# First head pair: two more blocks from unstacked parts, rotation of the rest on GpSimd, and the first weight conversion spread over later steps

## The chip, the cores and the metric

The kernel runs on one core of a Trainium2 chip. The metric is the time of one execution on the device, in microseconds (us), as the median of several runs. The core has five engines that work side by side: TensorE (PE, matrix products and transposes), VectorE (DVE), ScalarE (ACT), GpSimd (POOL) and SyncE (SP, which here only issues transfers). Each runs its own instructions in order and waits on semaphores for the others.

## The reference

Attention over 4 batches of 8 heads, 576 positions of 64 values, with rotated Q and K, and then a gated feed-forward layer over the 2304 rows of 512 values that attention gives. All of it is float32.

```python
q_rot, k_rot = (rotate(q), rotate(k))
scores = scale * np.matmul(q_rot, k_rot.transpose(0, 1, 3, 2))
scores = scores - np.max(scores, axis=-1, keepdims=True)
attn = np.exp(scores)
attn = attn / (np.sum(attn, axis=-1, keepdims=True) + 1e-09)
x = np.matmul(attn, v)            # then heads side by side: (2304, 512)
g = x @ w_gate
out = (g * (1.0 / (1.0 + np.exp(-g))) * (x @ w_val)) @ w_out
```

## The kernel before

**Tiling.** The 32 heads are taken as 16 pairs. A pair has nine blocks of scores: blocks 0 to 7 are four groups of 128 queries for either head in turn, block 8 holds the last 64 queries (the tails) of both heads. Blocks are numbered through, n = 9p + b, so block 9 is the first of pair 1. TensorE works on a fast float32 form, so each operand is split into a high and a low part, and a product of two operands is three products: high by high, low by high, high by low.

**A pair's way.** `load_qk` (L180) brings Q, K and the tails into a tile X, `load_v` (L195) brings V into VR. The rotation (`rope`, L198, its inner `part`, L206) is done in three groups: 0 is Q, 1 is K, 2 the tails. A group is four elementwise operations: two with the sines (L224, half the width each), one with the cosines (L227) and one addition (L228). `qk_T` (L291) transposes a group on TensorE, ScalarE writes the high part (`qk_hi`, L317), VectorE subtracts for the low part (`qk_lo`, L320), both into the tile N. `qk_stack` (L324) then copies parts of N by eight transfers into the stacked tiles QK, QZ and BD, in which high and low parts stand above one another, so that one product over 128 rows does the work of two over 64. `vsplit` (L284) makes the high and the low part of V on GpSimd.

**A block's way.** `scores` (L339) makes the products of a block: in the first pair the blocks below `ndir` straight from N, three terms of 64 rows (six instructions); the others from the stack (four instructions; block 8 six). `peak` (L367, the reduction at L375) takes the negated row maxima on VectorE, `exp` (L377, L393) the exponentials with their sums on ScalarE, `trans` (L416) transposes them on TensorE, ScalarE and VectorE again write high and low parts (L437, L438). `tails` (L440) does so for the last columns and queues the products with V, which `pv_some` (L503) hands out, so many a step, as `PLAN["pv"]` says; `pv_evac` copies a finished sum out. Two score buffers, three transpose buffers and one for the products with V exist.

**The start.** `start` (L238) does the first two blocks by hand, in an order that is kept on all engines: VectorE rotates K and then the first quarter of Q, GpSimd the tails; TensorE transposes them, with warm-up products between; then VectorE rotates the other three quarters of Q, blocks 0 and 1 are scored, the rest of Q is transposed, and the stack is copied, three of its six large copies from ScalarE's queue and the rest from SP's.

**The steps.** Then follows one step per block number n (the loop behind L1080). In a step the functions named in `PLAN["order"]` are called: `qk` transposes the next pair's groups at the blocks in `qk0`/`qk`, `scores` and `exp` belong to block n + 1, `trans` to block n - 1, `rope` rotates the pair after the next at block 1, `vsplit` stands at block 8. GpSimd keeps the written order throughout. On TensorE, ScalarE, VectorE and SP a planner puts the instructions in order by its own estimate of times, with the written order as the priority; only instructions wrapped in `keep_in_program_order` are pinned. One group of pair 1's rotation (K) is given to VectorE (`rv=[[1, 1]]`) and called at step 2.

**Weights and inputs of the second part.** `wfirst` (L748) loads one of the first two weight tiles (gate, value) and gives nine conversion steps each (`bits9`, L717): six on VectorE, one on ScalarE, two on GpSimd. `cl` says at which block numbers the loads are made, `cvs` at which of them the eighteen steps are called. The loads go to the single buffer R of `r_p`. In the later pairs the same buffer takes the reciprocal sums (`rload`, L619), four chunks at once, by which `xprep` (L641) on GpSimd multiplies the attention results that come back from memory.

Behind the attention part, up to the end, TensorE does the feed-forward products, with a hand-kept order on all engines.

## Time and profile before

| what | value |
|---|---|
| median of 3 runs | 727.87 us (725.9 to 728.76) |
| the profiled execution | 726.62 us, its span 724.8 us |
| TensorE busy in the span | 699.9 us (97%) |
| VectorE busy | 550.2 us (76%) |
| GpSimd busy | 465.8 us (64%) |
| ScalarE busy | 405.6 us (56%) |
| mean granted clock of TensorE | 0.989 of full speed |

The span runs from the first to the last instruction; what lies around it makes up the rest of the execution's time. A share of busy time is a mean over stages with different limits, so the start of the kernel is read by itself: by stretches of the span, by the chain of waits that ends there, and by the instructions in order of time. The maxima of the blocks (L375) serve as landmarks, since every block has one.

### The profile page before, as it was taken

Reading aid. Unit: us, or ns where it says so; the run is one execution under the profiler, and the core shown is the slowest. Engines: PE = TensorE matmul, PEld = TensorE weight load, DVE = VectorE, ACT = ScalarE, POOL = GpSimd, SP = SyncE. Lnnn points to the kernel's source line nnn. Section 1 sums busy time; section 2 is a strip of 40 time slices with the busy share of each in tenths; the row PEclk is TensorE's granted clock in tenths of the full one; section 3 lists DMA queues with packets and bytes.
Section 4 is the critical chain, followed back from the end, with each engine's and each line's share of the span. In section 5 each row is a group of like instructions: output and inputs, shape, how many; then the busy total and the mean of one; then the engine's idle time right before and its main releaser. Section 6 shows DMA issues by size and latency. Waiting matters only on the chain.

```text
span 724.8 us, 12728 instructions
## 1 busy us (share of the span) xinstructions
PE 699.9 (97%) x4356; PEld 658.8 (91%) x4356; DVE 550.2 (76%) x898; ACT 405.6 (56%) x884; POOL 465.8 (64%) x462
## 2 busy tenths in 40 slices
PE   7699999999999999998989999999999999999997
PEld 6589999999999999997989999999999877888887
DVE  5899888888888889657988868777766894365451
ACT  2688888888888888447543443414334342432331
POOL 5696989999899957576976766556764757200000
PEclk9899999999999999999999999999999999999999
DMA  5887778789887886793347564745547974786671
GB/s 172 223 198 222 200 195 240 199 205 251 217 205 207 229 203 202 201 262 124 118 143 199 162 191 134 202 147 175 161 145 229 305 263 158 291 290 234 203 218 30
DMA packets 111585, 144.12 MB, mean 199 GB/s; under 512 B 17808, under 2 KB 86432, under 8 KB 111520
## 3 DMA queue, kind: packets, MB, share of 16 engines
q1 hardware_dynamic: 106816, 137.51, 66.1%
q10 hardware_dynamic: 4704, 5.79, 2.4%
q8 instruction: 35, 0.57, 0.3%
q14 instruction: 30, 0.25, 0.1%
HBM read 76.61 MB, written 42.54 MB: 164 GB/s over the span
## 4 chain that ended last, share of the span: by engine, by line
PE 69%; DVE 13%; DMA 8%; ACT 6%; issue 1%; POOL 1%; SPq 1%; ACTq 0%; DVEq 0%
PE ch L822 28%; PE ch L939 13%; PE pv L476 10%; PE sc L360 9%; PE tr L436 7%; DMA HF<-hf 2%; DVE nmt L375 2%; PE tr L299 2%; ACT E L393 1%; DMA ht<-sv 1%; DVE HF L880 1%; ACT N L318 1%; POOL fl L695 1%; DMA QZ<-N 1%; DMA hg<-ht 1%
## 5 line engine op out<-in xcount | busy, mean ns | idle before, releaser
L375 DVE TENSOR_REDUCE nmt<-sc 128x1 f32<-128x576 f32 x144 | 107.9, 751 | 19.7 <-PE sc L360 18.4
L393 ACT ACTIVATE E<-sc,nmt 128x576 f32<-128x576 f32 x128 | 97.4, 761 | 9.7 <-DVE nmt L375 8.3
L436 PE MATMUL tr<-ident,E 128*128 128x128 f32 x512 | 77.2, 274 | 0.6 <-DVE N L322 0.6
L806 POOL TENSOR_TENSOR u<-u,z 128x384 f32<-128x384 f32 x30 | 30.5, 1016 | 73.2 <-DVE sg L806 70.8
L360 PE MATMUL sc<-QK 128*128 128x288 f32 x248 | 61.9, 331 | 4.2 <-DMA QK<-N 2.8
L436 PEld LDWEIGHTS tr<-ident,E 128*128 128x128 f32 x512 | 61.7, 141 | 2.6 <-PE tr L299 1.3
L825 ACT COPY c<-ch 128x384 f32<-128x384 f32 x30 | 14.4, 480 | 83.9 <-PE ch L822 49.4
L224 POOL TENSOR_TENSOR t<-X,tabs 128x256 f32<-128x256 f32 (+1 forms) x90 | 52.0, 600 | 14.4 <-DMA X<-in_qk_dram 7.2
L695 DVE TENSOR_TENSOR hl<-hg,hh 128x384 fp32r<-128x384 f32 x44 | 25.8, 587 | 39.2 <-ACT hh L695 39.2
L360 PE MATMUL sc<-N,QZ 128*128 128x288 f32 x248 | 54.0, 300 | 0.7 <-DMA QZ<-N 0.7
L939 PE MATMUL ch<-Oh,hh 128*128 128x512 f32 (+1 forms) x144 | 54.0, 375 | 0.1
L437 ACT CAST ET2h<-tr 128x512 fp32r<-128x512 f32 x80 | 47.1, 589 | 12.4 <-PE tr L436 12.4
L939 PE MATMUL ch<-Oh,hl 128*128 128x512 f32 (+1 forms) x144 | 53.9, 374 | 0.0
L939 PE MATMUL ch<-Ol,hh 128*128 128x512 f32 (+1 forms) x144 | 53.8, 374 | 0.0
L438 DVE TENSOR_TENSOR ET2l<-tr,ET2h 128x512 fp32r<-128x512 f32 x80 | 53.0, 682 | 0.6 <-ACT ET2h L437 0.6
L438 DVE TENSOR_TENSOR ET1l<-tr,ET1h 128x512 fp32r<-128x512 f32 x64 | 42.8, 685 | 7.5 <-ACT ET1h L437 7.4
L228 POOL TENSOR_TENSOR rot<-rot,t 128x512 f32<-128x512 f32 (+1 forms) x45 | 45.8, 1018 | 3.5
L437 ACT CAST ET1h<-tr 128x512 fp32r<-128x512 f32 x64 | 36.4, 598 | 18.2 <-PE tr L436 15.0
L360 PEld LDWEIGHTS sc<-QK 128*128 128x128 f32 x248 | 38.7, 193 | 8.1 <-ACT E L393 4.9
L806 DVE TENSOR_TENSOR sg<-ch,u 128x384 f32<-128x384 f32 x60 | 33.4, 557 | 16.2 <-PE ch L822 13.3
L227 POOL TENSOR_TENSOR rot<-X,tabs 128x512 f32<-128x512 f32 (+1 forms) x45 | 45.5, 1012 | 0.0
L695 ACT CAST hh<-hg 128x384 fp32r<-128x384 f32 x44 | 22.6, 514 | 38.8 <-DVE hg L926 38.8
(411 smaller groups left out, 2420.3 us busy)
## 6 DMA issues: line engine op xcount, KB each, us to landing
QK<-N SPq DMA_DIRECT2D x62, 288.0 KB, 5.0
hg<-ht SPq DMA_DIRECT2D x22, 768.0 KB, 6.1
HF<-hf SPq DMA_DIRECT2D x12, 896.0 KB, 5.1
X<-in_qk_dram SPq DMA_DIRECT2D x15, 576.0 KB, 6.7
yd<-Y SPq DMA_DIRECT2D x31, 256.0 KB, 4.0
ht<-sg SPq DMA_DIRECT2D x20, 384.0 KB, 3.6
hf<-sg SPq DMA_DIRECT2D x20, 384.0 KB, 3.6
ht<-sg SPq DMA_DIRECT2D x20, 320.0 KB, 2.9
```

The lines of the kernel that those rows point to most:

```text
L224: ins = e.tensor_tensor(out=sel(t2, u), in0=sel(x, w), in1=tb(Sn, u), op=ALU.mult)
L360: nc.tensor.matmul(ps[:, g, 0:288], l, rr[:, o + g * 288:o + (g + 1) * 288], start=(x == 0), stop=(x == len(terms) - 1))
L375: nc.vector.tensor_reduce(out=nmcol, in_=ps[:, :, 0:288], axis=AX.XY, op=ALU.max, negate=True)
L393: nc.scalar.activation(out=E.rearrange("p (a b) -> p a b", a=2), in_=ps[:, :, 0:288], func=ACTF.Exp, bias=nmcol, scale=1.0, accum_out=self ...
L436: nc.tensor.transpose(ps[:, c], E[:, o + c * 128:o + (c + 1) * 128], self.ident)
L437: nc.scalar.copy(dst[0], src)
L438: nc.vector.tensor_tensor(out=dst[1], in0=src, in1=r32(dst[0]), op=ALU.subtract)
L476: nc.tensor.matmul(st["ps"][:, 0:w], VS[:, sl, :], t, start=(x == 0), stop=(x == last))
L695: return [lambda: self.nc.scalar.copy(h, f), lambda: le.tensor_tensor(out=l, in0=f, in1=r32(h), op=ALU.subtract)]
L806: add = lambda e, out, in0, in1: e.tensor_tensor(out=out, in0=in0, in1=in1, op=ALU.add)
L822: nc.tensor.matmul(acc, l[:, w, c * 128:(c + 1) * 128], r, start=(n == 0), stop=(n == 5))
L939: self.nc.tensor.matmul(ps, l[:, f], r[:, z], start=(n == 0), stop=(n == 3 * NFF - 1))
```

## The change

- `ndir` goes from 4 to 6: blocks 4 and 5 of pair 0 are also made from the unstacked parts.
- In the start, the other three quarters of Q of pair 0 are rotated by GpSimd, behind the tails. The group of pair 1 that VectorE had goes to GpSimd too; GpSimd takes pair 1's groups in the order Q, tails, K, later pairs' in the order tails, Q, K.
- V is loaded ahead of pair 1's X. Pair 2's X is loaded inside the start, before the stack copies. The stack copies are all issued by SP.
- The high part of V of pair 0 is copied by ScalarE in the start; GpSimd makes the low part only.
- In the start, ScalarE writes the high part of the rest of Q before its first exponential.
- In the first nine steps TensorE too keeps the written order (`ctl1`), and the products with V are handed out by a list of their own (`pv0`): ten at step 6, ten at step 7, two at step 8.
- Pair 1's groups are transposed at blocks 3, 4 and 5 (Q, tails, K) of pair 0, pair 2's at blocks 1, 2 and 3 of pair 1.
- The conversion of the first weight tiles: loads at blocks 9 and 67 and not 0 and 9; the eighteen steps between blocks 12 and 104 and not 2 and 28.
- The reciprocal sums are loaded in halves of two chunks into a buffer of their own (`Rh`); R stays with the weight tiles up to block 104.

```diff
-    ndir=4,
+    ndir=6,
-    rv=[[1, 1]],
-    rl=2,
-    qk0=[2, 4, 4],
-    qk=[0, 0, 1],
-    qkw0=[0, 1, 2],
-    qkw=[2, 0, 1],
+    qk=[[3, 4, 5], [1, 2, 3], [0, 0, 1]],
+    qkw=[[0, 2, 1], [2, 0, 1], [2, 0, 1]],
     pv=[1, 6, 5, 3, 7, 8, 2, 7, 3],
+    pv0=[0, 0, 0, 0, 0, 0, 10, 10, 2],
-    cl=[0, 9],
-    cvs=[2, 2, 3, 3, 4, 4, 5, 6, 8, 12, 14, 16, 18, 20, 22, 24, 26, 28],
+    cl=[9, 67],
+    cvs=[12, 18, 24, 30, 36, 42, 48, 54, 60, 72, 76, 80, 84, 88, 92, 96, 100, 104],
...
+    def rope(self, p, order=(2, 0, 1)):
+        self.rot[p] = self.rot_p.tile([128, NSLOT, D], FP32, name="rot")
+        for g in order:
+            self.turn(self.nc.gpsimd, p, g)
+        del self.X[p]
...
-        for x in STARTS[PLAN["st"]]:
-            part((ve, po)[x[0]], *x[1:])
+        self.turn(ve, 0, 1)
+        self.turn(po, 0, 2)
+        self.turn(ve, 0, 0, 0, 1)
+        self.turn(po, 0, 0, 1, 4)
...
+        nc.scalar.copy(self.VS[0][:, :, 0:64], self.VR)
         warm(PLAN["warm"][1])
-        part(ve, 0, 0, 2, 1, 4, own=False)
...
         warm(PLAN["warm"][3])
+        hi(ps[:, 128:512], 192, 384)
         self.exp(0)
         self.peak(1)
-        hi(ps[:, 128:512], 192, 384)
         lo(ps[:, 128:512], 192, 384)
         self.exp(1)
+        del self.rot[0], self.X[0]
+        self.load_qk(2)
         self.qk_stack(0)
-        del self.rot[0]
...
-        nc.gpsimd.tensor_scalar(out=VS[:, :, 0:64], in0=VR, scalar1=1.0, scalar2=1.0, op0=ALU.mult, op1=ALU.mult)
+        if p:
+            nc.gpsimd.tensor_scalar(out=VS[:, :, 0:64], in0=VR, scalar1=1.0, scalar2=1.0, op0=ALU.mult, op1=ALU.mult)
...
-        e = d if p else self.nc.scalar.dma_start
-        e(out=QK[U, 1], in_=pair(N[V, 0, 0:576], QH + 576))
-        e(out=QK[V, 1], in_=pair(N[V, 1, 0:576], 576))
-        e(out=QZ[V, 1], in_=N[V, 1, 64:576])
+        d(out=QK[U, 1], in_=pair(N[V, 0, 0:576], QH + 576))
+        d(out=QK[V, 1], in_=pair(N[V, 1, 0:576], 576))
+        d(out=QZ[V, 1], in_=N[V, 1, 64:576])
...
         at.load_qk(0)
+        at.load_v(0)
         at.load_qk(1)
-        at.load_v(0)
         at.start()
-        at.load_qk(2)
...
-    at.rope(1)
+    at.rope(1, (0, 2, 1))
...
-        at.pv_some(P["pv"][b])
+        at.pv_some(P["pv" if p else "pv0"][b])
...
-            if c == 0:
-                moe.rload(s, t)
+            if c % 2 == 0:
+                moe.rload(s, t, at.rh_p.tile([128, 2 * BK], FP32, name="Rh"), c, 2)
...
+    ctl1 = tc.manual_schedule(engines={mybir.EngineType.PE})
+    ctl1.__enter__()
     for n in range(NB):
         p, b = divmod(n, 9)
+        if n == 9:
+            ctl1.__exit__(None, None, None)
```

## Rows read from the trace of the kernel before

**Rows 1.** Chain of waits, first 60 us: start us, us, what.

```profile
8.94 0.42 DVE Et L224
9.36 0.60 DVE rot L227
...
11.03 0.53 DVE t L224 x2
...
12.06 0.56 DVE rot L228
...
16.00 6.16 DMA QZ<-N
```

**Rows 2.** Instructions in order of time, first 46 us: start us, us, engine, line.

```profile
6.98 0.78 POOL L228 TENSOR_TENSOR rot<-rot,t 128x128 f32<-128x128 f32 x1
...
12.76 1.41 POOL L224 TENSOR_TENSOR t<-X,tabs 128x256 f32<-128x256 f32 x2 [5.00 <-DVE rot L228]
...
14.12 1.28 POOL L227 TENSOR_TENSOR rot<-X,tabs 128x512 f32<-128x512 f32 x1
...
15.44 1.17 PE L360 MATMUL sc<-N 64*128 64x288 f32 x12
...
16.81 0.66 PE L299 MATMUL tr<-ident,rot 128*128 128x128 f32 x4 [0.20 <-POOL rot L228]
16.83 0.60 POOL L224 TENSOR_TENSOR t<-X,tabs 128x64 f32<-128x64 f32 x2
...
18.35 0.72 POOL L288 TENSOR_SCALAR VS<-VR 128x640 fp32r<-128x640 f32 x1
...
19.69 0.59 ACT L318 CAST N<-tr 128x512 fp32r<-128x512 f32 x1
...
20.31 0.69 DVE L322 TENSOR_TENSOR N<-tr,N 128x512 fp32r<-128x512 f32 x1 [0.52 <-ACT N L318]
...
20.69 0.82 PE L360 MATMUL sc<-QK 128*128 128x288 f32 x2 [2.79 <-DMA QK<-N]
...
26.11 2.00 POOL L224 TENSOR_TENSOR t<-X,tabs 128x256 f32<-128x256 f32 x2 [5.41 <-DMA X<-in_qk_dram]
```

**Rows 3.** VectorE in order of time: maxima of blocks 9, 18, 36, 54.

```profile
36.74 0.74 DVE L375 TENSOR_REDUCE nmt<-sc 128x1 f32<-128x576 f32 x1
...
54.68 0.74 DVE L375 TENSOR_REDUCE nmt<-sc 128x1 f32<-128x576 f32 x1
...
87.52 0.76 DVE L375 TENSOR_REDUCE nmt<-sc 128x1 f32<-128x576 f32 x1 [0.21 <-PE sc L360]
...
120.80 0.76 DVE L375 TENSOR_REDUCE nmt<-sc 128x1 f32<-128x576 f32 x1 [0.21 <-PE sc L360]
```

**Rows 4.** Stretches: length, busy us of each engine, TensorE clock, DMA share, GB/s.

```profile
10.00:40.00 30.00, 22.52 (x155) 19.32 (x154) 24.19 (x39) 15.88 (x39) 20.43 (x24) 0.89 0.66 178
46.00:63.00 17.00, 16.45 (x128) 15.50 (x127) 16.72 (x26) 14.42 (x38) 16.37 (x19) 1.00 0.84 210
63.00:80.00 17.00, 16.86 (x135) 16.39 (x135) 16.25 (x27) 15.46 (x40) 10.69 (x14) 1.00 0.69 180
114.00:131.00 17.00, 16.89 (x135) 16.48 (x134) 14.94 (x24) 15.13 (x40) 15.54 (x19) 1.00 0.83 209
```

**Rows 5.** Stretches, TensorE alone: length, busy us, granted clock, DMA share, GB/s.

```profile
17.00:20.20 3.20, 0.90 (x8) 0.96 1.03 280
20.20:27.00 6.80, 5.53 (x21) 0.52 0.94 263
```

**Rows 6.** Transfer issues, first 50 us: count, KB each, median us to landing.

```profile
QK<-N SPq DMA_DIRECT2D x10, 288.0 KB, 4.3
```

**Rows 7.** SP in order of time, 112 to 114 us.

```profile
112.87 1.49 SPq L334 DMA_DIRECT2D QK<-N  x1
```

**Rows 8.** Groups by line, VectorE, first 46 us: busy us, mean ns.

```profile
L738 DVE SCALAR_TENSOR_TENSOR R<-R 128x512 uint32<-128x512 uint32 x1 | 1.6, 1616 | 0.0
...
L739 DVE TENSOR_SCALAR R<-R 128x512 uint32<-128x512 uint32 x1 | 0.6, 578 | 0.0
```

More of the change, by code (lines that the diff above doesn't have):

```diff
@@ new lines, in turn @@
+    def turn(self, e, p, g, ra=0, rz=4):
+        X, rot = self.X[p], self.rot[p]
+        C, Sn = self.tab[:, 0], self.tab[:, 1]
+        m = rz - ra
+        if e is self.nc.vector:
+            tt = self.et_p.tile([128, 640], FP32, name="Et")[:, 0:512].rearrange("p (s d) -> p s d", d=D)
+        else:
+            tt = self.t_p.tile([128, 8, D], FP32, name="t2")
+        if g < 2:
+            x = X[:, 8 * g:8 * g + 8].rearrange("p (h r) d -> p h r d", r=4)[:, :, ra:rz]
+            o = rot[:, 8 * g:8 * g + 8].rearrange("p (r h) d -> p h r d", h=2)[:, :, ra:rz]
+            tb = lambda t, u: t[:, None, 5 - 5 * g + ra:5 - 5 * g + rz, u].to_broadcast([128, 2, m, u.stop - u.start])
+            t2 = tt[:, 0:m * 2].rearrange("p (h r) d -> p h r d", r=m)
+            sel = lambda t, u: t[:, :, :, u]
+        else:
+            x, o = X[:, 16:18], rot[:, 16:18]
+            tb = lambda t, u: t[:, 4:5, u].to_broadcast([128, 2, u.stop - u.start])
+            t2 = tt[:, 0:2]
+            sel = lambda t, u: t[:, :, u]
+        for u, w in ((slice(0, HALF), slice(HALF, D)), (slice(HALF, D), slice(0, HALF))):
+            e.tensor_tensor(out=sel(t2, u), in0=sel(x, w), in1=tb(Sn, u), op=ALU.mult)
+        e.tensor_tensor(out=o, in0=x, in1=tb(C, slice(0, D)), op=ALU.mult)
+        e.tensor_tensor(out=o, in0=o, in1=t2, op=ALU.add)
@@ L617, in aux, with rload @@
         return self.aux_p.tile([128, 512], FP32, name="aux")
-    def rload(self, s, t, into=None):
-        R = self.r_p.tile([128, NCH * BK], FP32, name="R") if into is None else into
-        R = R.rearrange("p (c n) -> p c n", c=NCH)
+    def rload(self, s, t, R, c0=0, nc=NCH):
+        R = R.rearrange("p (c n) -> p c n", c=nc)
         b0, b1 = 2 * s, 2 * s + 1
```

62 lines of the change are left out of this document (10 added, 52 removed), and 4 rows, old and new, of the table STARTS.

## The prediction

> **What bounds the kernel now.** I read the stretches first, then the chain of waits, then the timeline of the first 46 us. In a stretch from the middle of the attention part TensorE is busy for 16.89 of 17.00 us [rows 4]: from there on nothing but TensorE's own work sets the time, and an edit elsewhere is free as long as it fits beside. The first pair differs. From 10 to 40 us TensorE is busy for 22.52 of 30 us [rows 4], warm-up products included, so 7.48 us are idle. The row maxima show the same: between the first maximum of pair 1 (block 9) and that of pair 2 (block 18) lie 54.68 - 36.74 = 17.94 us, while the two pairs from block 18 to block 36 take 87.52 - 54.68 = 32.84, or 16.42 each [rows 3]. At that pace a block costs 16.42 / 9 = 1.83 us. Pair 1 is thus 1.52 over the pace, and pair 0 ends far over it.
>
> The chain of waits names the causes in pair 0. Up to the first maximum it is VectorE: two operations of pair 1's K rotation have slid in between (8.94 to 9.96), and the rest of pair 0's Q rotation stands ahead of the maximum (11.03 to 12.62) [rows 1]. Then it is the stacked copies: 6.16 us for the QZ copy issued at 16.00, which lands at 22.16 [rows 1], with TensorE idle for 2.79 us before block 4 at 20.69 [rows 2]. The clock falls behind that idleness: granted 0.52 from 20.2 to 27.0, nearly all of it at the lower level of 1.2 GHz, after a stretch in which TensorE had been busy for 0.90 of 3.20 us [rows 5]. After that the conversion of the first weight tiles fills VectorE: 16.72 of 17 us from 46 to 63 [rows 4].
>
> **The change, part by part.** I count back from the landmark of block 9's maximum (36.74) and block 18's (54.68), since behind block 18 TensorE is full and a shift there is carried to the end.
>
> *Start.* Off VectorE go the two slid operations, 0.42 + 0.60 = 1.02, and the rest of Q, from 11.03 to 12.06 + 0.56 = 12.62, 1.59 [rows 1]. The chain could shrink by 2.61, at the least by 1.02. Blocks 2 and 3 start at 15.44 [rows 2]; they now wait for the rest of Q from GpSimd. That price the trace does not show at this size. GpSimd takes 1.41 / 2 = 0.70 for 128x256 and 1.28 for 128x512 [rows 2], so by size two operations of 128x192 cost 0.53 each and two of 128x384 0.96 each: 2.98, behind the tails' turn that ends at 6.98 + 0.78 = 7.76. That gives 10.74; behind it still stand three transposes and the eight warm-up products. I take 1.7 of gain, block 2 at 13.7 (bounds 12.8 and 14.4). The copy of V's high part on ScalarE lies where the chain is VectorE's throughout [rows 1], with ScalarE waiting for the first maximum, and costs nothing; without that cover it costs one operation, about the 0.72 of GpSimd's own copy at 18.35 [rows 2]. Loading V ahead of pair 1's X delays that X, but GpSimd reads it from 10.7 on only.
>
> *Blocks 4 and 5 from parts.* Twelve products of the unstacked form took 1.17 us for two blocks [rows 2], so a block is about 0.6 to 0.7; four products more than from the stack, some 0.3 us in all. In return the wait of 2.79 and the one for QZ go. The stack is first needed at block 6. At the steady pace that is 13.7 + 4 x 1.83 = 21.0. The three copies that leave ScalarE's queue stand behind three others on SP, and behind the load of pair 2's X, which itself waits for GpSimd's 10.74. With 4.3 us from issue to landing as the median [rows 6] and 6.16 as the slow case the copies for block 6 land between 19 and 21.5: at most half a microsecond is lost. What is late next is pair 1.
>
> *Pair 1 from GpSimd.* All three groups are now GpSimd's, in its order: 10.74 + Q group (0.70 + 0.70 + 1.28 + 1.28 = 3.96) + tails (16.83 to 18.35, 1.52) + K group (3.96) = 20.2 [rows 2]; with some lengthening, since the same two operations took 2.00 at 26.11 and 1.41 at 12.76, I take 20.8. Then four transposes (0.66), the high part (0.59), the low part (0.69) [rows 2], on SP one copy ahead of the low part's (about 0.6) and 4.3 from issue to landing [rows 6]: 27.6. With half a microsecond for the queue it is 28.1 for block 9, and its maximum at 28.8. By pace alone block 9 would be reached at 13.7 + 7 x 1.83 = 26.5, so this chain, not TensorE, is what is late. Against 36.74 that gives 8.0 us. Bounds: the pace, 27.2, gives 9.5; GpSimd's 12 us stretched by a fifth (2.4) and 6.16 for the landing (1.9) give 33.1, or 3.6.
>
> *Pair 1 itself* took 17.94 with conversion steps on VectorE; only one step of eighteen is left in it, at block 12. Between 16.42 and 17.94 I take 17.4, another 0.5 (bounds 0 and 1.5). Pair 2's X is issued before the stack and not at 20 us, so GpSimd need not wait for it before 26.11 [rows 2]; its 9.4 us of rotation end near 32, when pair 1 asks for it at its blocks 1 to 3.
>
> *Conversion over pairs 1 to 11.* Eighteen steps, of which twelve are VectorE's, four GpSimd's. They cost nothing as long as VectorE has room: 14.94 of 17 us are used in the middle [rows 4], 2.06 are free, and a pair gets one and a half to two steps. In favour: from 63 to 80 VectorE was busy for 16.25 of 17 us and those pairs kept the pace of 16.42. *The halved loads of the reciprocals* wait for GpSimd's multiplication of the chunk before; behind them on SP stand stores and the next stack. Pair 6's last stack copy is issued at 112.87 [rows 7] and its first maximum comes at 120.80 [rows 3], so SP has some 4 us of room after landing: nothing.
>
> Sum: 8.0 + 0.5 = 8.5 us (bounds 3.6 and 11.0). The profiled execution took 726.62, its span 724.8; the median of the runs, 727.87, is 1.25 above it. 726.62 - 8.5 = 718.1, beside the median 719.4, which I forecast.
>
> **One rule against the change.** GpSimd's operations are stretched at times: the same two took 1.41 at 12.76 and 2.00 at 26.11, 0.59 more [rows 2]. The Trainium skill, page "SBUF — State Buffer", section "SBUF: two separate sides", gives a reason: GpSimd and VectorE share a port pair, which is an exclusive lock for a whole instruction when VectorE reads two operands from SBUF; whoever comes second waits. By that rule GpSimd's turn of the rest of Q, which begins beside VectorE's four operations on Q's first quarter, would wait perhaps twice; at 0.59 each, an estimate, that makes 1.2, and the sum would be 7.3, 720.6 beside the median. VectorE's later work in the first pair reads one operand from PSUM, so the rule asks no more there. I leave the sum as it is.
>
> **Rivals.** (a) The wait moves. TensorE, held in written order, stands before block 9 as it stood before block 4, and the clock falls again. Nearly 7 us at the lower level in a stretch that is otherwise full cost half of it, 3.4 us: 8.5 - 3.4 = 5.1, 722.8. For it: the wait before block 9 in my own count is 1.6 us. Against it: it is shorter than the 2.79, with products on either side.
> (b) The written order eats the gain. Before, the planner could put ready products of P and V into a gap; now nothing may overtake the transposes that wait for GpSimd, and the 7.48 us of idleness stay as they are, only elsewhere. Then only the start's 1.7 to 2.6 are left: 725.3 to 726.2, no change that shows. Against it: GpSimd begins 2.0 us earlier than its first turn of pair 1 at 12.76 and does not stop for X.
> (c) Slower: the conversion lands on TensorE's path. Each of the twelve VectorE steps takes 0.58 to 1.62 [rows 8], 1.1 as the middle, and if each delays a maximum while TensorE has nothing else queued, pairs 1 to 11 lose 12 x 1.1 = 13.2: 727.87 - 8.5 + 13.2 = 732.6. It decides from where a step is longer than what VectorE has free between two maxima, 2.06 / 9 = 0.23 a block if nothing is queued ahead; the two score buffers speak against it, and the pairs from block 18 on, which carried steps at the full pace.
>
> **How the numbers follow.** Forecast 719.4, with 717 to 721.5 for itself: 0.60. (a), or the lower bounds of pair 1's chain (3.6 gives 724.3): 0.20. (b): 0.11. (c): 0.09. A measurement of this kernel tells apart about 0.5%, 3.6 us. The forecast and (a) lie beyond that on the fast side: 0.80; (b) is within: 0.11; (c) slower: 0.09. The range goes from 716.5 (the whole of 11.0 us) to 724.3 and leaves out (b) and (c).
>
> **What would show it.** Right: block 2 near 13.7, no wait on a QK or QZ copy before block 4, block 9's maximum at 28 to 30, block 18's at 45 to 47, later pairs at 16.4 to 16.7, granted clock full after 20 us. Wrong: TensorE waiting long for GpSimd's rotation or a QK copy before block 9 (then (a) or (b)); pairs 2 to 11 over 17 us with VectorE's conversion lines as the releaser (then (c)).

## The result and the profile after

The changed kernel takes 735.9 us (median; 732.2 to 738.0), the kernel before 727.6 beside it: a ratio of 1.011 [1.0065, 1.0156]. It is slower by 8.3 us where I had forecast 8.5 us of gain.

The maxima of the blocks tell where. VectorE in order of time, the kernel after, the maxima of blocks 9, 18, 108, 135 and 143 (the last), beside [rows 3]; then the kernel before, blocks 108, 135 and 143:

```profile
35.68 0.76 DVE L355 TENSOR_REDUCE nmt<-sc 128x1 f32<-128x576 f32 x1 [2.51 <-PE sc L340]
...
56.44 0.76 DVE L355 TENSOR_REDUCE nmt<-sc 128x1 f32<-128x576 f32 x1 [0.49 <-PE sc L340]
...
225.94 0.76 DVE L355 TENSOR_REDUCE nmt<-sc 128x1 f32<-128x576 f32 x1 [0.21 <-PE sc L340]
...
275.55 0.76 DVE L355 TENSOR_REDUCE nmt<-sc 128x1 f32<-128x576 f32 x1 [0.20 <-PE sc L340]
...
295.08 0.74 DVE L355 TENSOR_REDUCE nmt<-sc 128x1 f32<-128x576 f32 x1
```

```profile
219.80 0.76 DVE L375 TENSOR_REDUCE nmt<-sc 128x1 f32<-128x576 f32 x1 [0.21 <-PE sc L360]
...
269.39 0.76 DVE L375 TENSOR_REDUCE nmt<-sc 128x1 f32<-128x576 f32 x1 [0.20 <-PE sc L360]
...
285.69 0.74 DVE L375 TENSOR_REDUCE nmt<-sc 128x1 f32<-128x576 f32 x1
```

Between the two profiled executions (spans 734.1 and 724.8, 9.3 apart) the account is:

| stretch, by maxima | before | after | difference |
|---|---|---|---|
| up to block 9 | 36.74 | 35.68 | -1.06 |
| pair 1 (blocks 9 to 18) | 17.94 | 20.76 | +2.82 |
| pairs 2 to 11 | 165.12 | 169.50 | +4.38 |
| pairs 12 to 14 | 49.59 | 49.61 | +0.02 |
| pair 15, to its block 8 | 16.30 | 19.53 | +3.23 |
| behind the last maximum | 439.11 | 439.02 | -0.09 |

**The start.** Instructions in order of time, after, with what ended the wait ahead of them in brackets:

```profile
7.98 0.76 DVE L207 TENSOR_TENSOR Et<-X,tabs 128x64 f32<-128x64 f32 x2 [0.59 <-DMA tabs<-in_rope_dram]
8.05 1.16 POOL L207 TENSOR_TENSOR t<-X,tabs 128x192 f32<-128x192 f32 x2 [0.34 <-DMA tabs<-in_rope_dram]
8.66 0.69 DVE L208 TENSOR_TENSOR rot<-X,tabs 128x128 f32<-128x128 f32 x1
9.17 1.04 POOL L208 TENSOR_TENSOR rot<-X,tabs 128x384 f32<-128x384 f32 x1
9.39 0.97 DVE L209 TENSOR_TENSOR rot<-rot,Et 128x128 f32<-128x128 f32 x1
...
10.41 0.33 PE L241 MATMUL tr<-ident,rot 128*128 128x128 f32 x1 [1.68 <-DVE rot L209]
...
19.00 1.06 PE L340 MATMUL sc<-N 64*128 64x288 f32 x6
...
19.74 1.27 POOL L209 TENSOR_TENSOR rot<-rot,t 128x512 f32<-128x512 f32 x1
...
26.06 0.60 PE L280 MATMUL tr<-ident,rot 128*128 128x128 f32 x4
...
34.88 0.50 PE L340 MATMUL sc<-QK 128*128 128x288 f32 x2 [1.86 <-DMA QK<-N]
...
37.42 0.82 PE L340 MATMUL sc<-QK 128*128 128x288 f32 x2 [1.03 <-DMA QK<-N]
```

VectorE's four operations on Q's first quarter and GpSimd's on the rest end in turn: GpSimd's first pair ends at 9.21, VectorE's operation from 8.66, whose like took 0.28 before, at 9.35; GpSimd's next ends at 10.21, VectorE's at 10.36. VectorE takes 2.38 us for the four. TensorE waits 1.68 us for it. Block 2, forecast at 13.7, begins at 19.00. Then blocks 2 to 8 run without a wait on a stack copy, as intended, and blocks 9 and 10 each wait for a QK copy (1.86 and 1.03 us). GpSimd ends pair 1's last group, K, at 21.01; the transposes of that group stand at block 5 in TensorE's written order and come only at 26.06, and the QK copies are issued behind them.

Stretches, after (length, busy us of the engines, granted clock, share of the transfer engines, GB/s), in the order PE, PEld, DVE, ACT, POOL:

```profile
11.90:18.80 6.90, 6.90 (x35) 6.12 (x34) 1.98 (x3) 1.94 (x5) 6.59 (x11) 0.52 0.32 101
24.70:34.90 10.20, 8.00 (x63) 7.19 (x61) 7.34 (x13) 7.99 (x21) 9.88 (x12) 1.00 0.95 229
35.80:42.70 6.90, 5.87 (x27) 5.44 (x26) 4.17 (x7) 3.45 (x9) 6.66 (x8) 0.52 0.37 122
```

The clock is at the lower of its two levels, 1.2 GHz, twice: behind the wait for VectorE's quarter and behind the wait before block 9. In the first stretch TensorE is busy throughout, but mostly with products at half speed. Before there was one such stretch [rows 5].

### The profile page after: what moved, and what is told of

Same layout as the page of the kernel before. It is cut to its first block, busy times and chain, and to the rows that moved or that the text cites. A ratio compares the mean times of both kernels' runs of the same rounds, so it can differ in the third digit from the quotient of the medians.

```text
span 734.1 us, 12779 instructions
## 1 busy us (share of the span) xinstructions
PE 704.9 (96%) x4360; PEld 662.7 (90%) x4360; DVE 546.9 (74%) x890; ACT 408.4 (56%) x885; POOL 470.9 (64%) x469
## 3 DMA queue, kind: packets, MB, share of 16 engines
q1 hardware_dynamic: 107344, 138.24, 66.1%
## 4 chain that ended last, share of the span: by engine, by line
PE 75%; DVE 8%; DMA 7%; ACT 4%; SPq 2%; issue 2%; POOL 1%; ACTq 0%; DVEq 0%
PE ch L801 27%; PE ch L918 12%; PE pv L456 10%; PE sc L340 10%; PE tr L416 7%; PE ch L869 3%; DMA HF<-hf 2%; PE ch L753 2%; PE tr L280 2%; DVE nmt L355 1%; DMA ht<-sv 1%; DMA raw<-in_moe_w_gate_dram 1%; ACT E L373 1%; DVE ET2l L418 1%; DVE HF L859 1%
## 5 line engine op out<-in xcount | busy, mean ns | idle before, releaser
L373 ACT ACTIVATE E<-sc,nmt 128x576 f32<-128x576 f32 x128 | 97.1, 759 | 11.1 <-DVE nmt L355 10.2
L804 ACT COPY c<-ch 128x384 f32<-128x384 f32 x30 | 14.4, 480 | 83.9 <-PE ch L801 45.7
L207 POOL TENSOR_TENSOR t<-X,tabs 128x256 f32<-128x256 f32 (+2 forms) x94 | 54.2, 599 | 4.5 <-DMA X<-in_qk_dram 1.7
L417 ACT CAST ET2h<-tr 128x512 fp32r<-128x512 f32 x80 | 47.1, 589 | 16.2 <-PE tr L416 15.7
L209 POOL TENSOR_TENSOR rot<-rot,t 128x512 f32<-128x512 f32 (+2 forms) x47 | 47.7, 1015 | 3.7
L208 POOL TENSOR_TENSOR rot<-X,tabs 128x512 f32<-128x512 f32 (+2 forms) x47 | 47.5, 1010 | 0.0
L785 DVE TENSOR_TENSOR sg<-ch,u 128x384 f32<-128x384 f32 x60 | 33.4, 557 | 16.2 <-PE ch L801 13.0
```

Of the source, the lines that this page charges most:

```text
L207: e.tensor_tensor(out=sel(t2, u), in0=sel(x, w), in1=tb(Sn, u), op=ALU.mult)
L373: nc.scalar.activation(out=E.rearrange("p (a b) -> p a b", a=2), in_=ps[:, :, 0:288], func=ACTF.Exp, bias=nmcol, scale=1.0, accum_out=self ...
L417: nc.scalar.copy(dst[0], src)
L785: add = lambda e, out, in0, in1: e.tensor_tensor(out=out, in0=in0, in1=in1, op=ALU.add)
```

## The experiments

All medians stand beside the kernel before on the same chip (726.7 to 727.9). Landmarks are of the profiled execution: first maximum, those of blocks 9 and 18, and the time of pairs 2 to 11 and of pair 15.

| run | median us | ratio to before | first | block 9 | block 18 | pairs 2-11 | pair 15 |
|---|---|---|---|---|---|---|---|
| before | 727.6 | 1 | 12.54 | 36.74 | 54.68 | 165.12 | 16.30 |
| after | 735.9 | 1.011 [1.0065, 1.0156] | 14.72 | 35.68 | 56.44 | 169.50 | 19.53 |
| b_halves | 732.8 | 1.0065 [1.0045, 1.0084] | 13.99 | 38.64 | 56.37 | 164.97 | 19.88 |
| b_conv | 735.6 | 1.011 [1.0075, 1.0146] | 14.06 | 37.63 | 55.44 | 167.43 | 20.57 |
| a_onlystart | 722.1 | 0.9938 [0.9916, 0.9959] | 13.73 | 33.87 | 52.49 | 164.84 | 15.98 |
| a_convearly | 729.0 | 1.0017 [0.9997, 1.0037] | 12.77 | 33.06 | 52.41 | 164.79 | 18.84 |
| a_convoff | 730.2 | 1.0037 [1.0017, 1.0056] | 12.56 | 33.83 | 52.20 | 164.32 | 22.98 |
| e_pause | 731.5 | 1.0072 [1.0041, 1.0103] | 13.31 | 34.08 | 53.04 | 166.90 | 20.93 |
| e_lastwhole | 727.3 | 0.9997 [0.9974, 1.002] | 12.66 | 33.54 | 52.39 | 168.58 | 15.84 |
| a_qafter | 734.4 | 1.0108 [1.0063, 1.0153] | 12.09 | 34.11 | 51.80 | 169.33 | 22.18 |
| d_q_sp | 731.1 | 1.0048 [1.0029, 1.0066] | 12.75 | 32.95 | 50.83 | 168.85 | 20.14 |
| d_q_x3sp | 731.1 | 1.0049 [1.0032, 1.0066] | 12.01 | 30.29 | 49.52 | 168.27 | 21.83 |
| c_start_q | 723.4 | 0.9948 [0.9927, 0.9969] | 11.92 | 32.70 | 51.91 | 165.35 | 15.80 |
| c_start_q_x3 | 724.1 | 0.9954 [0.994, 0.9968] | 12.47 | 33.83 | 55.77 | 164.53 | 15.91 |
| d_dummy | 724.9 | 0.9963 [0.9945, 0.9981] | 12.21 | 33.06 | 52.42 | 166.31 | 16.00 |
| d_best | 721.7 | 0.9926 [0.9905, 0.9947] | 14.44 | 34.82 | 53.99 | 165.53 | 16.18 |
| e_best2 | 722.5 | 0.9946 [0.9929, 0.9963] | 11.85 | 29.54 | 47.63 | 169.20 | 16.73 |
| e_best3 | 721.6 | 0.9913 [0.9898, 0.9928] | 12.15 | 29.87 | 48.48 | 166.50 | 15.99 |

The start of a single execution varies by itself: the first loads land up to 1.2 us later in one than in another (VectorE's first operation begins at 4.92 in after, at 6.08 in d_q_sp), and in some VectorE then waits up to 1.19 us more for the rest of the sines and cosines (tabs). The block 9 column is to be read with the first maximum beside it. Each row's landmarks are those of one execution, while its median is of several.

### The parts apart: reciprocals, conversion, start

**b_halves**: the kernel before, with the reciprocal sums in halves.

```diff
...
-            if c == 0:
-                moe.rload(s, t)
+            if c % 2 == 0:
+                moe.rload(s, t, at.rh_p.tile([128, 2 * BK], FP32, name="Rh"), c, 2)
...
```

> The kernel before with one part of the change: the reciprocals come in halves of two chunks into a buffer of their own; the conversion stays where it was. Theory (the halves cost SP's order and GpSimd's wait, 3.2 us in pair 15): 730 to 731.5 us, block 135 to 143 takes about 19.5 instead of 16.3, the weight tile of that pair is loaded after 280 us, and GpSimd waits about 10 us for the second half. Rival (the late load comes from the conversion's new place): within 1 us of before, 16.3 stays.

**b_conv**: that, and the conversion at its new place.

```diff
-    cl=[0, 9],
+    cl=[9, 67],
...
+    cvs=[12, 18, 24, 30, 36, 42, 48, 54, 60, 72, 76, 80, 84, 88, 92, 96, 100, 104],
```

> The kernel before with two parts of the change: the halves, and the conversion spread over blocks 12 to 104; the first pair's work is that of before. Theory (each long conversion step on VectorE delays a maximum): pairs 2 to 11 take 168.5 to 169.5 instead of 165.1 us, so 3 to 4.4 us on top of the halves' 3.2: 733 to 735.5, less what pairs 0 and 1 win by losing the steps (up to 3). Rival (the 4.4 us of pairs 2 to 11 are a consequence of the first pair's new order): 165 to 166 there, the whole at 728 to 731.

**a_onlystart**: the changed kernel with both of these as before, so that only the work on the first pairs is new.

```diff
-    cl=[9, 67],
+    cl=[0, 9],
...
-            if c % 2 == 0:
-                moe.rload(s, t, at.rh_p.tile([128, 2 * BK], FP32, name="Rh"), c, 2)
+            if c == 0:
+                moe.rload(s, t, moe.r_p.tile([128, NCH * BK], FP32, name="R"))
...
```

> The changed kernel with conversion and reciprocals as before: only the first pair's work is the changed one. Theory (conversion and halves cost 7.6 us together): pairs 2 to 11 at 165 to 166, pair 15 at 16.3 to 16.6, the whole at 727 to 731, since the conversion's steps come back into pairs 0 and 1, which stay slower at the start. Rival (the losses behind block 18 come from the first pair's order): 734 to 736.

**a_convearly**: the changed kernel with only the conversion put back (`cl` and `cvs` as before).

> The changed kernel with the conversion at its old place (loads at blocks 0 and 9, steps at blocks 2 to 28), the halved reciprocals kept. If the later place of the conversion costs pairs 2 to 11 their 4.4 us, these take 164.9 us, block 18's maximum comes 0 to 1 us later than in the changed kernel (56.4 to 57.4, as the steps return to pairs 1 and 2), pair 15 still takes 19 to 20 us, and the time is 731.5 to 732.5. If pairs 2 to 11 are slow for another reason (written order at the start, the rotation's order), they stay at 169 and the time at 736.

Measured: the halves cost 5.2 us in the old kernel (732.8 against 727.5) and 6.9 in the new one (729.0 against 722.1). The later conversion costs 2.8 (735.6 against 732.8) and 6.9 (735.9 against 729.0). The new start alone gains 5.4 (722.1 against 727.5), and with the halves 3.8 (729.0 against 732.8). Three expectations missed on the way: a_onlystart and a_convearly are faster than I expected (727 to 731 and 731.5 to 732.5), with block 18 at 52.4 to 52.5, where I had expected 56.4 to 57.4 in a_convearly; and in b_conv pairs 2 to 11 take 167.43 us, 2.5 more than in b_halves, between the theory's 168.5 and the rival's 166. So the first part of the change, which carried my whole sum, is a gain, and two edits that I had costed at nothing turn it into a loss. With the late conversion and the halves on both sides the start's gain is gone (735.9 against 735.6). The later runs show in part why.

### The conversion

**a_convoff**: the changed kernel without VectorE's twelve steps on the first weight tiles; the conversion of those tiles is left out. (The expectation says that ScalarE's two steps go too. They stay: its copies w0h and w1h are in the trace at 110.84 and 198.76.)

```diff
...
+        if bare:
+            Xf = Hf
+        return ([lambda: None] * 6 if bare else self.bits(raw, None, None, Xf if Xt is None else Xt, Xf)[:6]) + [
...
```

> The changed kernel without VectorE's and ScalarE's twelve plus two steps of the first weight tiles' conversion; GpSimd's four steps stay. The first tile of each weight matrix is thus not converted, and the output is not the reference's. If VectorE's steps delay the maxima, pairs 2 to 11 take 164.9 to 165.3 us instead of 169.5, with every pair at 16.4 to 16.6, and the time falls by some 4.5 to 731.4; pair 15 keeps its 19.5. If GpSimd's steps, or the loads of the weights, are what slows pairs 2 to 11, they stay at 168 to 169.5.

Pairs 2 to 11 take 164.32 us: the 5.2 us lie in VectorE's steps, not in ScalarE's, GpSimd's or the loads. The last maximum comes 5.9 us earlier and not 9.4, because pair 15 takes 22.98 (see below). What makes a step long the trace of after shows. VectorE and GpSimd in order of time, two long steps with the operation of GpSimd beside each, then a short one, and one from the end of the attention part:

```profile
73.18 1.31 POOL L208 TENSOR_TENSOR rot<-X,tabs 128x512 f32<-128x512 f32 x1
73.23 1.53 DVE L716 TENSOR_SCALAR R<-R 128x512 uint32<-128x512 uint32 x1
...
164.10 1.29 POOL L208 TENSOR_TENSOR rot<-X,tabs 128x512 f32<-128x512 f32 x1
164.12 1.55 DVE L713 TENSOR_SCALAR R<-R 128x512 uint32<-128x512 uint32 x1
...
62.86 0.42 DVE L715 TENSOR_SCALAR R<-R 128x512 f32<-128x512 f32 x1
...
292.28 0.41 DVE L716 TENSOR_SCALAR raw<-raw 128x512 uint32<-128x512 uint32 x1
```

These two steps begin while an operation of GpSimd runs and end 0.27 and 0.28 us behind its end (73.18 + 1.31 = 74.49, the step at 74.76). An operation of this kind takes 0.41 or 0.42 where GpSimd does nothing beside it. Of the twelve steps six take 1.32 to 1.80, one of them in pair 1 and five in pairs 2 to 11. The delay shows block by block against a_convoff: the two maxima around the step at 73.23 stand at 71.96 and 74.69, 2.73 apart, and in a_convoff 0.97; around the step of 1.80 at 107.69 they are 3.00 apart, in a_convoff 0.97. VectorE in a_convoff, the same two maxima as around 73.23:

```profile
66.86 0.76 DVE L355 TENSOR_REDUCE nmt<-sc 128x1 f32<-128x576 f32 x1 [0.43 <-PE sc L340]
67.83 0.76 DVE L355 TENSOR_REDUCE nmt<-sc 128x1 f32<-128x576 f32 x1 [0.21 <-PE sc L340]
```

Over blocks 49 to 72, which have none of VectorE's steps, the lag behind a_convoff stays at 3.7.

**e_pause**: the changed kernel with VectorE's six steps of the first tile moved into the stretches of pairs 2 and 3 in which GpSimd waits.

```diff
-    cvs=[12, 18, 24, 30, 36, 42, 48, 54, 60, 72, ...
+    cvs=[20, 21, 22, 29, 30, 31, 48, 54, 60, 72, ...
...
```

> The changed kernel with VectorE's six steps of the first tile at blocks 20, 21, 22, 29, 30 and 31 instead of 12 to 42, so that they fall into the 5 us in which GpSimd pauses in pairs 2 and 3; the second tile's steps stay. If a step costs TensorE only where it has to wait for an operation of GpSimd, the six last 0.4 to 0.7 us each and pairs 2 to 11 go from 169.5 to 165.5 to 167 us, pairs 8 and 9 keeping their 17.3 and 17.5; the time falls by 3 to 4. If it is VectorE's added work as such, six steps in two pairs cost as much as in four: pairs 2 to 11 stay at 169 or above, and pairs 2 and 3 take over 17.5 each.

```profile
61.95 0.42 DVE L713 TENSOR_SCALAR R<-R 128x512 uint32<-128x512 uint32 x1
...
64.64 1.59 POOL L270 TENSOR_TENSOR VS<-VR,VS 128x640 fp32r<-128x640 f32 x1
...
65.48 1.03 DVE L716 TENSOR_SCALAR R<-R 128x512 uint32<-128x512 uint32 x1
```

(VectorE and GpSimd in pair 2.) Five of the six steps take 0.42 to 0.80, the one that meets GpSimd 1.03. Pairs 2 to 5 together take 66.29 us, in a_convoff, without VectorE's steps, 65.28, in the changed kernel 68.97. So six steps in two pairs cost 1.0 us where five in four pairs cost 3.7: most of the cost is the place beside GpSimd and not the work itself. In e_best2 below, steps crowded into fewer blocks cost much more.

### The start and the two engines on Q

**a_qafter**: the changed kernel, GpSimd's rest of Q begins behind VectorE's quarter (VectorE writes one column of the tile that GpSimd needs).

```diff
...
+            if p == 0 and g == 0:
+                self.nc.vector.memset(tt[:, 0:1, 0:1], 0.0)
...
```

> The changed kernel with one small VectorE write into GpSimd's scratch tile, so that GpSimd's turn of the rest of Q begins only after VectorE's four operations on Q's first quarter. Theory (the two engines lock one another out of their shared port: VectorE's four took 2.38 us instead of 0.93, TensorE idled and the clock fell): VectorE's four take 0.9 to 1.0 again, blocks 0 and 1 run at the full clock, block 2 starts at 15.5 to 17.5 instead of 19.0, the whole is 2 to 3.5 us faster, 732 to 734. Rival (the late cosines, or the clock by itself): VectorE's four shrink, but block 2 stays at 18.5 to 19.5 and the time at 735 to 736.

Instructions in order of time, from the same four operations of VectorE, and block 9:

```profile
7.82 0.60 DVE L209 TENSOR_TENSOR Et<-X,tabs 128x64 f32<-128x64 f32 x2
...
8.66 0.29 DVE L211 TENSOR_TENSOR rot<-rot,Et 128x128 f32<-128x128 f32 x1
...
9.05 1.14 POOL L209 TENSOR_TENSOR t<-X,tabs 128x192 f32<-128x192 f32 x2 [0.85 <-DVE t L196]
...
32.77 0.82 PE L342 MATMUL sc<-QK 128*128 128x288 f32 x2 [4.51 <-DMA QK<-N]
```

VectorE's four take 1.13 us instead of 2.38, and TensorE's wait for them shrinks from 1.68 to 0.18. Block 9 comes only 1.6 us earlier, though: a wait of 4.51 for QK stands before it in one piece, and the clock is low from 31.9 to 38.7. The time hardly moves (734.4, where 732 to 734 were expected): block 18 comes 4.6 us earlier than in after, but pairs 2 to 11 still take 169.33 and pair 15 takes 22.18.

**c_start_q**: a_onlystart with that same edit.

> The new first pair alone (conversion and reciprocals as in the kernel before), and GpSimd's rest of Q begins only behind VectorE's first quarter. If the two engines' operations on Q lengthen each other and that alone made the start late, the four operations of VectorE take about 1.5 us (0.60, 0.28, 0.29) instead of 2.4, the first maximum comes at about 12.1 and block 18's at 50.0 to 50.9 us, with no later loss: 719.6 to 720.7 us. If block 9 waits for pair 1's stack whatever the start does (its transfers stand in SP's queue), block 9's maximum stays near 33.9, block 18's near 52.5, and the time at 722.

Block 2 begins at 14.38, where a_onlystart has 16.17. But block 9 gains 1.2 us of these 1.8, block 18 gains 0.6, and the median shows nothing (723.4 against 722.1, the intervals overlap). Again block 9 waits for QK (1.57 us).

Not all of the 1.8 us is the two engines' doing. In after, a_onlystart and e_pause VectorE waited 0.38 to 0.87 us for tabs, so that both engines began together, and VectorE's four took 2.38. In a_convoff, a_convearly and e_lastwhole (below), with the same work up to there, VectorE began first, and its four took 1.66 to 1.80. Counted from VectorE's first operation, block 2 begins after 9.8 us in these three and after 10.8 and 11.0 in e_pause and a_onlystart. In the eight runs with the edit in which no clock falls there it begins after 9.1 to 9.4. So the two engines at once cost 0.4 to 1.9 us, by who begins first.

The low clock at the start of after did not come back with the same work either. TensorE in e_pause, its wait for VectorE's quarter and block 2:

```profile
10.25 0.33 PE L241 MATMUL tr<-ident,rot 128*128 128x128 f32 x1 [1.80 <-DVE rot L209]
...
15.75 1.05 PE L340 MATMUL sc<-N 64*128 64x288 f32 x6
```

The wait is longer than the 1.68 of after, the granted clock stays at 1.00 from 11.9 to 18.8, and block 2 comes 3.3 us earlier.

### What block 9 waits for

In after, 24.70 to 34.90, the transfer engines are 0.95 busy. By then SP has issued pair 3's X (576 KB), pair 1's VR (320 KB) and pair 1's stack (four QK of 288 KB, two QZ of 128, two BD of 32: 1472 KB), 2368 KB or 2.42 MB; at 229 GB/s that is 10.6 us, and the stretch lasts 10.2. So bytes could set block 9.

**c_start_q_x3**: c_start_q with pair 3's load called at block 6 of pair 0.

```diff
...
-        if b == P["lqk"] and p + 3 < NP:
+        if b == (P["lqk"] if p else 6) and p + 3 < NP:
...
```

> As the run before, and the load of pair 3's Q and K (576 KB) is issued at block 6 of pair 0 instead of block 0, behind and not ahead of pair 1's stack copies. If that load is what makes the copies land 5.6 to 6.3 us after their issue, they land within 4.3 to 4.8 us, the maximum of block 9 comes 1 to 2 us earlier than in the run before, and the time is 718 to 719.5. If the landing time is the copies' own (six of them beside one another) or the wait stands ahead of their issue, block 9 stays within 0.3 us and so does the time.

This told nothing of the bytes: SP's planned order kept the load ahead of the copies (issued at 23.37 instead of 22.52). But its profiled execution gives a bound for the price of the clock: behind waits of 2.05 and 1.07 before blocks 9 and 10, instead of 1.57 and 0.64, the clock is low from 34.7 to 38.2, and pair 1 takes 21.94 instead of 19.21, 2.73 more. Of this 0.43 is the longer wait before block 10 (the wait before block 9 lies ahead of pair 1). The other 2.3 are more than half of these 3.4 us, 1.7; what the remaining 0.6 is stays open.

**d_q_sp**: a_qafter with SP in the written order over the first nine steps. **d_q_x3sp**: that, and pair 3's load at block 6, which is now really behind the copies.

```diff
-    ctl1 = tc.manual_schedule(engines={mybir.EngineType.PE})
+    ctl1 = tc.manual_schedule(engines={mybir.EngineType.PE, mybir.EngineType.SP})
```

> The changed kernel with GpSimd's rest of Q behind VectorE's quarter, and SP in the written order over the first nine steps: pair 3's load of 576 KB still stands ahead of pair 1's stack copies. This is the control for the next run. If bytes ahead in the full transfer engines set when the copies land, the wait before block 9 stays between 3.5 and 5 us, block 9's maximum at 33.5 to 34.5, the clock falls there as without the written order, and block 18's maximum is at 51 to 53 us. If the order among the copies themselves is what counts, block 9 moves by more than 1 us already here.

> As the control, and pair 3's load of 576 KB is issued behind pair 1's stack copies. By bytes: 576 KB at the 245 GB/s of that stretch are 2.35 us, so the wait before block 9 falls from about 4.5 to about 2.2 us, block 9's maximum comes at 31.2 to 32.2, and if the clock then does not fall, block 18's at 47.5 to 49.5 us. If the copies land late for another reason (issue, the copies among one another), block 9 stays within 0.4 us of the control.

TensorE and SP in order of time, first d_q_sp, then d_q_x3sp:

```profile
22.10 0.53 SPq L174 DMA_DIRECT2D X<-in_qk_dram  x1
...
31.66 0.71 PE L342 MATMUL sc<-QK 128*128 128x288 f32 x2 [2.78 <-DMA QK<-N]
```

```profile
29.27 0.50 PE L342 MATMUL sc<-QK 128*128 128x288 f32 x2 [1.08 <-DMA QK<-N]
...
31.29 0.59 SPq L174 DMA_DIRECT2D X<-in_qk_dram  x1
```

The control's block 9 moved by 1.16 us, just over the bound of 1 that I had set for the order among the copies, and by 1.8 against its own first maximum: the order counts too. (Its wait of 2.78 also misses the 3.5 to 5 that I had expected.) On top of it the 576 KB take 1.70 us off the wait, where 2.35 were expected, and no clock falls in the first 280 us. So the bytes ahead set block 9, along with the order of the copies. The median is the same (731.1): block 18 keeps 1.3 us of the gain, and pair 15, late by the reciprocals in both, takes 1.7 more.

**d_dummy**: c_start_q with one more load of 576 KB that nobody uses.

```diff
...
+        if p == 3:
+            d(out=self.dm_p.tile([128, NSLOT, D], FP32, name="DM"), in_=self.qk[p])
...
```

> The new first pair alone with GpSimd's rest of Q behind VectorE's quarter (conversion and reciprocals as before), and one more load of 576 KB, used by nobody, ahead of pair 3's. By bytes pair 1's copies land 2.2 to 2.6 us later: block 9's maximum at 34.9 to 35.3 instead of 32.7, with a longer wait for a QK copy, and the time at 724 to 727 (a fall of the clock included). If the transfer engines have room, block 9 stays within 0.5 us of 32.7 and the time at 722 to 724.

It tells nothing of the copies either: as no one waits for it, the planner issued it at 4.75 us, where there was room. Block 9 stays (33.06).

### Pair 15 and the reciprocals

SP, GpSimd, VectorE and TensorE in after, around pair 15; then SP in a_onlystart:

```profile
259.00 0.58 SPq L609 DMA_DIRECT2D Rh<-rd  x1
...
265.07 0.60 SPq L609 DMA_DIRECT2D Rh<-rd  x1
...
269.75 3.49 SPq L609 DMA_DIRECT2D Rh<-rd  x4
...
275.28 1.01 POOL L624 TENSOR_TENSOR Xab<-Xab,Rh 128x384 f32<-128x384 f32 x1 [12.66 <-DMA Rh<-rd]
...
284.30 0.55 SPq L732 DMA_DIRECT2D raw<-in_moe_w_gate_dram  x1
...
289.08 0.55 DVE L713 TENSOR_SCALAR raw<-raw 128x512 uint32<-128x512 uint32 x1 [4.26 <-DMA raw<-in_moe_w_gate_dram]
...
291.21 0.53 PE L340 MATMUL sc<-QK 128*128 128x288 f32 x2 [3.33 <-ACT E L373]
```

```profile
266.19 0.44 SPq L732 DMA_DIRECT2D raw<-in_moe_w_gate_dram  x1
```

The third group of chunks needs six transfers for each half. The first two are issued singly ahead of the last stack copies, the other four behind them; GpSimd waits 12.66 us for the last; the weight tile that VectorE converts in pair 15 is loaded behind them, at 284.30 (a_onlystart: 266.19); VectorE's pinned step waits for it, and the maximum and TensorE behind that. Behind TensorE's wait the clock is low from 291.6 to 295.0; it falls in pair 15 in each of the nine runs with halves to the end, and in no other. The wait also eats what the kernel gained before: in a_convoff pair 15 begins 9.4 us earlier, but the step that waits for the weight tile begins at 283.23, only 5.9 earlier, and pair 15 takes 22.98.

**e_lastwhole**: a_convearly with the reciprocals in whole for the last eight chunks.

```diff
...
+            if len(xq) < 8:
+                if c == 0:
+                    moe.rload(s, t, moe.r_p.tile([128, NCH * BK], FP32, name="R"))
+            elif c % 2 == 0:
...
```

> The changed kernel with the conversion at its old place, and the reciprocals of the last eight chunks (from pair 12 on) loaded in whole again, those of the first eight in halves. If pair 15 is late because GpSimd waits for the last halves and the weight tile's load stands behind them in SP's order, pair 15 takes 15.9 to 16.5 us instead of 18.8, and the time is 724 to 726. If the halves of the earlier pairs set it, pair 15 stays at 18.5 or more and the time at 729.

Pair 15 takes 15.84 us: its delay comes from the last halves. But pairs 9 and 10 now take 18.66 and 18.02, and the median, 727.3, is above what was expected. TensorE and SP there:

```profile
170.37 2.57 SPq L609 DMA_DIRECT2D R<-rd  x4
...
177.11 0.62 SPq L310 DMA_DIRECT2D QK<-N  x1
...
185.64 0.50 PE L340 MATMUL sc<-QK 128*128 128x288 f32 x2 [1.92 <-DMA QK<-N]
```

The first whole load (R) stands ahead of pair 10's stack copies on SP. The first QK copy is issued at 177.11, in a_convearly at 174.30; TensorE waits 1.92 us for a copy before pair 10, where a_convearly has no wait, and behind the wait the clock is low from 186.4 to 189.8.

### All costs taken away together

**d_best**: c_start_q, SP in the written order over the first nine steps, pair 3's load and pair 1's V at block 6.

```diff
...
-        if b == P["lv"] and p + 1 < NP:
+        if b == (P["lv"] if p else 6) and p + 1 < NP:
...
```

> The new first pair alone, GpSimd's rest of Q behind VectorE's quarter, SP in the written order over the first nine steps, and pair 3's Q and K and pair 1's V both loaded behind pair 1's stack copies (896 KB moved). By bytes block 9's maximum comes 2 to 3.5 us before 32.7, at 29.2 to 30.7, and block 18's at 48.5 to 50: 719 to 721 us. If VectorE's conversion steps in pair 0 are then what is late, block 9 gains less than 1 us and the time stays at 722 to 723.5.

**e_best2**: that, with the conversion out of pair 0.

```diff
+    cl=[9, 26],
+    cvs=[11, 12, 20, 20, 21, 22, 23, 24, 25, 29, 29, 30, 31, 38, 38, 39, 40, 41],
...
```

> The new first pair with GpSimd's rest of Q behind VectorE's quarter, SP in the written order over the first nine steps, pair 3's Q and K and pair 1's V behind pair 1's stack copies, the reciprocals as before, and the conversion out of pair 0: most of VectorE's steps in GpSimd's pauses of pairs 2 to 4. If the conversion steps in pair 0 cost block 9 some 2 us and steps in GpSimd's pauses cost nothing, block 9's maximum comes at 29.5 to 31, block 18's at 48.5 to 50.5, pairs 2 to 11 take 165 to 166.5, and the time is 718.5 to 721. If the first pairs are bound by their transfers whatever VectorE does, block 18 stays at 52 and the time at 722.

**e_best3**: that start, one conversion step a block, meant for GpSimd's pauses, the reciprocals in halves for the first four chunks alone.

```diff
+    cl=[9, 35],
+    cvs=[20, 21, 22, 29, 30, 31, 32, 33, 34, 38, 39, 40, 47, 48, 49, 50, 52, 53],
...
+            if len(xq) < 12:
...
```

> The start of the run before (GpSimd's rest of Q behind VectorE's quarter, SP in the written order over the first nine steps, pair 3's Q and K and pair 1's V behind pair 1's stack copies), with the conversion one step a block in GpSimd's pauses of pairs 2 and 3, the second tile's in pairs 4 and 5, and the reciprocals in halves for the first four chunks, in whole from then on. If the four costs found are all there is between the forecast and the changed kernel, block 9's maximum comes at 29.5 to 30.5, block 18's at 47 to 48, pairs 2 to 11 take 165.3 to 167, pair 15 takes 16 to 16.5, and the time is 717.5 to 720. If conversion steps or the whole loads cost elsewhere what they no longer cost there, pairs 2 to 11 take 168 or more, or pair 15 18 or more, and the time is 721 to 725.

d_best kept nine conversion steps in pair 0, six of them VectorE's; its block 9 comes 20.4 us behind the first maximum, hardly less than in c_start_q (20.8), in e_best2 and e_best3 17.7; of the 2.7 between them some 1.7, an estimate, are a low clock from 27.4 to 30.9 in d_best. e_best2 failed its expectation: pairs 2 to 11 take 169.20 us, not 165 to 166.5. Pairs 2 and 3, with eight of VectorE's steps in them, take 37.20 against 32.12 in a_convoff, though only two of these steps take over 1 us. VectorE and GpSimd there, one of the two:

```profile
58.51 1.25 DVE L719 SCALAR_TENSOR_TENSOR R<-R 128x512 uint32<-128x512 uint32 x1
...
59.17 1.73 POOL L210 TENSOR_TENSOR rot<-X,tabs 128x512 f32<-128x512 f32 x1
```

GpSimd was not pausing: it rotates without a break from 53.6 to 62.4, and VectorE has no idle time from 56.6 to 66.1. So a pause planned from one kernel's trace had moved in the next. That steps crowded on a full VectorE delay the blocks without being long themselves is the likely reading, but no run tests it apart. With one step a block (e_best3) pairs 2 to 11 take 166.50, still 2.2 more than in a_convoff.

The maxima of e_best3, blocks 9, 18 and the last:

```profile
29.87 0.76 DVE L357 TENSOR_REDUCE nmt<-sc 128x1 f32<-128x576 f32 x1 [1.40 <-PE sc L342]
...
48.48 0.76 DVE L357 TENSOR_REDUCE nmt<-sc 128x1 f32<-128x576 f32 x1 [0.27 <-PE sc L342]
...
280.51 0.74 DVE L357 TENSOR_REDUCE nmt<-sc 128x1 f32<-128x576 f32 x1
```

Block 9's maximum, forecast at 28.8, is there at 29.5 to 29.9, and block 18's, forecast at 46.2, at 47.6 to 48.5. e_best3 ends the attention part 5.2 us before the kernel before and 2.4 before a_onlystart. d_best's median, 721.7, is above the 719 to 721 expected; e_best3's, 721.6, misses the 717.5 to 720 that I had expected and is still that of a_onlystart and d_best: behind the last maximum it takes 439.3 us, they 437.0 and 437.1. Why the feed-forward part gives back 2.3 us is open; about half of it (1.2 us against a_onlystart) is lost in the first 50 us of that part. The three are the fastest versions, 5.4 to 6.3 us under before, and cannot be told apart.

## Why the prediction was wrong

The forecast of 719.4 failed by 16.5 us. By medians the part that carried the sum, the new start, was right in kind and short in size: alone it gains 5.4 us (a_onlystart) of the 8.5, within the bounds 3.6 and 11.0. The two edits that the sum put at nothing cost 13.8 us together (735.9 against 722.1). They are the steps that failed: the conversion's "they cost nothing as long as VectorE has room" and the halves' "some 4 us of room after landing: nothing".

By the landmarks of the two profiled executions: block 9 came at 35.68 instead of 28.8 (6.9 late), pair 1 took 20.76 instead of 17.4 (3.4), pairs 2 to 11 4.4 more than before where I had nothing, and pair 15 3.2 more where I had nothing. That is 17.9, the forecast's 8.5 of gain and the 9.3 of loss.

- **The conversion: wrong, rival (c) in a smaller size.** I counted 2.06 us of room in 17, and what mattered most was whether GpSimd runs beside a step. [rows 8] already showed it: 1.616 us for an operation whose like takes 0.68 alone. The Trainium skill, page "SBUF — State Buffer", section "Who interferes with whom", counts operations of one tensor and a scalar among those that can take the shared port pair, and the traces agree (0.41 or 1.53 us); I had applied its rule to operations with two operands from SBUF only. The twelve steps cost 4.4 to 5.2 us in pairs 2 to 11, not the 13.2 of (c): only five of the steps there met GpSimd for long.
- **The halved reciprocals: wrong.** The room behind [rows 7] was there for the stack (TensorE waits for no copy in pairs 14 and 15 of after), but the queue behind the halves holds the next weight tile, and the third group needs six transfers a half. This edit alone costs 5.2 to 6.9 us, as much as the conversion's new place (2.8 to 6.9) or more.
- **Start: wrong by what I set aside, and then unlucky.** Block 2 was to come at 13.7. With GpSimd behind VectorE's quarter it comes at 14.4 to 14.6 (c_start_q, a_qafter), with the two engines on Q at once at 15.0 to 16.2 in five variants. In after it came at 19.00: some 3 us of that are the low clock behind TensorE's wait, which e_pause, with the same work, did not have. GpSimd's own work had the right size (3.20 us against 2.98). The Trainium skill, page "SBUF — State Buffer", section "SBUF: two separate sides", had named the cause, and the 1.2 us that I worked out by it lie within the measured 0.4 to 1.9; I took nothing, and looked at GpSimd's side of the lock, while VectorE, on the path, bore the wait.
- **Blocks 4 and 5 from parts: right.** Blocks 2 to 8 take 11.3 us from maximum to maximum (20.09 to 31.43) without a wait for a stack copy; the wait of [rows 2] is gone.
- **Pair 1 from GpSimd: the rotation right, the rest of the chain late.** GpSimd's chain ended at 21.0 (forecast 20.2 to 20.8). I then let TensorE transpose at once. In after it did so at 26.06, 5.1 us later, since the transposes stand at block 5 in the written order and the start was late: 5.3 of block 9's 6.9 us came this way. From these transposes to block 9 I had counted 7.3 us (20.8 to 28.1); it took 8.8 in after and 10.7 in a_qafter, whose start was mended (22.07 to 32.77). What failed there is "4.3 from issue to landing" [rows 6] and half a microsecond for the queue: the QK copies took 5.2 us in the median (14 to 40 us), among 2.4 MB queued. With 576 KB fewer ahead and SP in the written order (d_q_x3sp) it is 7.3 (21.99 to 29.27). [rows 5] showed the transfer engines 0.94 to 1.03 busy in the first pair; I took a landing from a list and not from the bytes.
- **Rival (a) came true as well**: the wait moved before block 9 and the clock fell there. In after and in four of its variants with conversion late and pair 3's load ahead (a_qafter, a_convoff, d_q_sp, e_pause) it is low in a stretch between 31.8 and 42.8. In a_onlystart, a_convearly and c_start_q, whose pair 0 has conversion steps in it, the waits are split and it does not fall there; in c_start_q_x3, with them, it does, and in e_lastwhole and d_best it falls earlier, from 26.0 and 27.4. Its price cannot be read from pair 1's length: without a fall in it pair 1 takes 18.1 to 19.4, with one 17.7 (a_qafter) to 21.9. Half of after's 6.9 us would be the 3.4 that I gave it, an estimate; c_start_q_x3 allows at most 2.3 for 3.4 us.
- **Pair 1 itself** takes 18.1 to 19.4 us in the nine runs with the new start in which no clock falls within it, not 17.4: its second block waits another 1.0 us for QK in after and about as long in several of them.
- **Small slips in the sum:** 36.74 less 28.8 is 7.9 and not 8.0, and 11.0 off 727.87 is 716.9 and not 716.5. Nothing hangs on either.

## What to carry to other kernels

Where the transfer engines are full, work out a landing from the bytes queued ahead and their rate, and put the load that is needed last behind the copies that are needed first. A VectorE step that is "free" by its busy share is cheaper where GpSimd pauses, if the pause is looked for in the new kernel's own trace and the steps are not crowded into it; its length in a trace with GpSimd beside it is mostly waiting. A transpose in a written order waits for its place as well as for its input. An edit that only makes room for another (here smaller buffers) has to be costed by what stands behind it in its queue.
